# A first stage in another order: the third attention unit ahead of the second up step, and weight conversion further ahead

## The chip, the cores and the metric

The kernel runs on one core of one Trainium2 chip. The metric is the device time of one execution in microseconds (us). The engines are TensorE (PE in the profile, PEld for its weight loads), VectorE (DVE), ScalarE (ACT), GpSimd (POOL) and SyncE (SP, which issues most transfers). Each has a program of its own.

## The reference

A retention block without softmax feeds a multiplicative feed-forward network:

```python
scores = scale * np.matmul(q, k.transpose(0, 1, 3, 2))
ret = scores * Dmat[None, :, :, :]            # decay gamma ** (i - j) below the diagonal, 0 above
x = np.matmul(ret, v)                         # (8, 8, 576, 64), turned to (4608, 512)
a = x @ w1; b = x @ w2
out = ((a * b) @ w3) @ w_out                  # w1, w2: 512 x 1024; w3: 1024 x 1024; w_out: 1024 x 512
```

The weights come as float64: the kernel reads them as pairs of 32-bit integers and makes float32 of them itself.

## The kernel before

The sequence is cut into units of up to 128 positions (five to a pair of batches). A unit is loaded, its q and v are scaled on GpSimd (`scale`), q and k are transposed on TensorE and copied out by ScalarE (`front`), a running state is updated (`state`), scores are made on TensorE and masked on VectorE (`score`), and `pv` multiplies with v. The up step `up(pair, token block, weight part)` is a Strassen product: seven products on TensorE, adds on VectorE. It needs sums S1 to S4 of converted weight blocks; a weight part has four blocks. It also needs sums of x, the token sums, which `strassen_tokens` makes for each token block.

A block is converted in five steps, which a generator hands out wherever the kernel calls `convert(n)`:

```python
def begin_block():                             # three steps
    vec.tensor_scalar(out=e, in0=hi, ...)      # exponent field
    yield
    vec.tensor_scalar(out=m, in0=hi, ...)      # mantissa, high part
    yield
    vec.scalar_tensor_tensor(m, in0=lo, ..., in1=m)
    nc.scalar.activation(e, e, relu, ...)      # two activations on ScalarE
    nc.scalar.activation(e, e, relu, ...)
    yield

def end_block():                               # two steps; after the fourth block of a part, the sums too
    vec.scalar_tensor_tensor(e, in0=hi, ..., in1=e)
    yield
    vec.scalar_tensor_tensor(out, in0=m, ..., in1=e)
    ...                                        # next load; strassen_weights
    yield

def conversion():
    yield from begin_block()
    while converted[0] < len(blocks):
        if begun[0] < len(blocks):
            yield from begin_block()
        yield from end_block()
```

`conv=2` in an up step hands out two conversion steps after each of its adds and at its end. The adds go through one tile `c` with a single buffer: ScalarE copies the first product into it, VectorE adds the others, multiplies (`ab`), and only then can the next up step use it.

Of the kernel before, what the change touches and what calls it, by code (L numbers as in the profile page):

```python
# [32 lines left out]
def kernel(  # L33
# [124 lines left out]
    def scale(g, nm):  # L158
        c = g % NC
        sz = sizes[c]  # L160
        t, gam = live[nm, g], {"q": gq, "v": gk}[nm]
        t = t[:sz].rearrange("p (b h) d -> p b h d", b=2)
        nc.gpsimd.tensor_tensor(  # L163
            out=t, in0=t, in1=gam[:sz, c].unsqueeze(1).unsqueeze(3).to_broadcast([sz, 2, H, D]), op=ALU.mult)

    def front(g):
        c = g % NC
        sz = sizes[c]
        kn, qn = live["k", g], live["q", g]
        kT = pools["fr"].tile([P, 2, NP, P], F32, tag="kT", name="kT", bufs=1)  # L170
        qT = pools["fr"].tile([P, 2, NP, P], F32, tag="qT", name="qT")
        for src, dst in ((kn, kT), (qn, qT)):
            for b in range(2):
                tp = acc.tile([P, NP, P], F32, tag="acc", name="tp")
                for p in range(NP):
                    h = b * H + 2 * p
                    nc.tensor.transpose(tp[:, p, :sz],  # L177
                                        src[:sz, h:h + 2, :].rearrange("p a d -> p (a d)"),
                                        ident[:sz, :sz])
                nc.scalar.copy(dst[:, b, :, :sz], tp[:, :, :sz])  # L180
        live["kT", g], live["qT", g] = kT, qT
# [17 lines left out]
    def state(g):  # L199
        c = g % NC  # L200
        sz = sizes[c]
        if c == NC - 1:
            return
        kn, vs = live["k", g], live["v", g]
        if c == 0:
            live["st"] = st_ps.tile([P, 2, NP, D], F32, tag="st", name="st")
        st = live["st"]

        for b in range(2):
            for p in range(NP):  # L210
                for j, hs in enumerate(heads):
                    h = b * H + 2 * p + j
                    nc.tensor.matmul(st[hs, b, p, :], kn[:sz, h, :], vs[:sz, h, :],  # L213
                                     start=(c == 0 and b == 0 and p == 0), stop=(c == NC - 2),
                                     skip_group_check=True)
        sb = pools["fr"].tile([P, 2, NP, D], F32, tag="sb", name="sb")
        nc.scalar.copy(sb, st)
        live["sb", g + 1] = sb
# [32 lines left out]
    blocks = []  # L251
# [7 lines left out]
    loaded, begun, converted, turned = [0], [0], [0], [0]  # L259
# [23 lines left out]
    def converted_to(n):  # L283
        key, _ = blocks[n]
        if key[0] == "w12":
            _, fp, j, r = key
            return wA[fp // 2][:, j, 2 * r:2 * r + 2, fp % 2 * QC:fp % 2 * QC + QC]
        if key[0] == "wo":
            return live["wo"][:, key[1], :]
        _, ft, g0 = key  # L290
        if ("w3", ft) not in live:
            live["w3", ft] = pools["wst"].tile([P, DF], F32, tag="w3", name="w3")
        return live["w3", ft][:, g0:g0 + CV]

    def begin_block():
        n = begun[0]
        t = live["raw", n]
        lo, hi = t[:, :, 0], t[:, :, 1]
        e = raw.tile([P, CV], I32, tag="exp", name="e")
        m = raw.tile([P, CV], I32, tag="man", name="m")  # L300
        vec = nc.vector


        vec.tensor_scalar(out=e, in0=hi, scalar1=1, scalar2=21,  # L304
                          op0=ALU.logical_shift_left, op1=ALU.logical_shift_right)
        yield

        vec.tensor_scalar(out=m, in0=hi, scalar1=0x000FFFFF, scalar2=0x00100000,
                          op0=ALU.bitwise_and, op1=ALU.bitwise_or)
        yield  # L310
        vec.scalar_tensor_tensor(m.bitcast(F32), in0=lo.bitcast(U32), scalar=2.0 ** -32, in1=m,  # L311
                                 op0=ALU.mult, op1=ALU.add)
        relu = mybir.ActivationFunctionType.Relu
        nc.scalar.activation(e, e, relu, bias=lim[:, 0:1], scale=-1.0)  # L314
        nc.scalar.activation(e, e, relu, bias=lim[:, 1:2], scale=-2.0 ** 23)
        live["em", n] = e, m
        begun[0] += 1
        yield

    def end_block():  # L320
        n = converted[0]
        hi = live["raw", n][:, :, 1]
        e, m = live["em", n]
        vec = nc.vector
        vec.scalar_tensor_tensor(e, in0=hi, scalar=-(1 << 31), in1=e,  # L325
                                 op0=ALU.bitwise_and, op1=ALU.bitwise_or)
        yield
        key = blocks[n][0]
        while not (key[0] == "w12" or "wo" in live and (key[0] == "wo" or key[1] < turned[0] + 2)):
            yield "wait"  # L330
        out, m, e = converted_to(n), m.bitcast(F32), e.bitcast(F32)
        if key[0] == "w12":
            m, e = (x.rearrange("p (c n) -> p c n", c=2) for x in (m, e))
        vec.scalar_tensor_tensor(out, in0=m, scalar=2.0 ** -20, in1=e, op0=ALU.mult, op1=ALU.mult)  # L334
        converted[0] += 1

        if n > 0:
            load_block()
        if key[0] == "w12" and key[1] > 0 and key[2:] == (1, 1):
            yield from strassen_weights(key[1])  # L340
        yield

    def conversion():

        yield from begin_block()
        while converted[0] < len(blocks):
            if begun[0] < len(blocks):
                yield from begin_block()
            yield from end_block()

    converting = [conversion()]

    def go_on():
        while converting:
            r = next(converting[-1], "end")
            if r != "end":
                return r
            converting.pop()
        return "end"

    def convert(n):

        for _ in range(n):
            if go_on() is not None:
                return
# [28 lines left out]
    def has_x(i, n):  # L394
        return any(starts[c] + sizes[c] >= (n + 1) * TB and ("x", i * NC + c) in live for c in range(NC))
# [17 lines left out]
    def up(i, n, fp, conv=0):  # L413
        m = every.index((i, n))
        while ("S", fp) not in live:
            assert go_on() is None
        if ("B", i, n) not in live:
            strassen_tokens(i, n)
        if fp == 0:
            live["ab", i, n] = (pools["ab3"] if m == 2 else ffn).tile([P, 2 * KF, TB], F32, tag="ab", name="ab")  # L420
        ab = live["ab", i, n]

        def product(ps, a, b):
            a, b = A(fp, a), live["B", i, n][b]
            new = ps is None
            if new:
                ps = acc.tile([P, 2, TB], F32, tag="acc", name="up")
            for w in range(2):
                for r in range(2):
                    nc.tensor.matmul(ps[:, w, :], a[:, w, r, :], b[:, r, :], start=(new and w == r == 0),  # L430
                                     stop=(w == r == 1), skip_group_check=True)
            return ps

        def plus(ps, to, sb):
            nc.vector.tensor_add(c[:, to], ps, c[:, sb])  # L435
            convert(conv)


        c = ffn.tile([P, 4, 2, TB], F32, tag="c", name="c", bufs=1)
        p1 = product(None, "A11", "B11")  # L440
        nc.scalar.copy(c[:, 0], p1)  # L441
        plus(product(None, "S2", "T2"), 1, 0)
        plus(product(None, "S3", "T3"), 2, 1)
        p5 = product(None, "S1", "T1")
        plus(p5, 3, 2)
        plus(product(None, "A22", "-T4"), 2, 2)
        product(p1, "A12", "B21")
        nc.scalar.copy(c[:, 0], p1)  # L448
        product(p5, "S4", "B22")
        plus(p5, 1, 1)  # L450

        if fp == NQ - 1 and m + 1 < len(every) and has_x(*every[m + 1]) and ("B", *every[m + 1]) not in live:
            strassen_tokens(*every[m + 1])
        nc.vector.tensor_mul(ab[:, 4 * fp:4 * fp + 4, :], c[:, :, 0, :], c[:, :, 1, :])  # L454
        convert(conv)
# [43 lines left out]
    scale(1, "q")  # L499
    front(1)  # L500
    scale(1, "v")
    state(1)
    score(1)
    convert(2)
    pv(1)
    strassen_tokens(0, 0, nc.vector)
    load(3, "kqv")
    up(0, 0, 0, conv=2)
    scale(2, "q")
    scale(2, "v")  # L510
    up(0, 0, 1, conv=2)
    front(2)
    state(2)
    score(2)
    load(4, "k")
    scale(3, "q")
    front(3)
    scale(3, "v")
    load(4, "q")
    state(3)  # L520
    score(3)
# [1 line left out]
    load(4, "v")  # L523
    pv(3)
    strassen_tokens(0, 1, nc.vector)
    convert(2)
    up(0, 1, 0, conv=2)
    scale(4, "q")
    scale(4, "v")
# [136 lines left out]
```

## Time and profile before

| | |
|---|---|
| time, median of 6 runs | 938.4 us (937.4 to 939.0) |
| span of the profiled run | 935.2 us |
| TensorE busy | 899.6 us (96%) |
| TensorE idle from 0 to 30 us, where DMA is full | 15.9 us |
| TensorE idle from 40 to 60 us, where VectorE is full | 10.7 us |

The last two rows are the lengths of the windows less TensorE's busy time in them; the prediction shows the windows. Besides these large gaps TensorE has small ones later; three of them are of one kind. This is its order in time (start us, duration us, engine, line, operation, matrices, count; in brackets the idle time ahead of the group and who ended it):

```profile
108.31 1.57 PE L430 MATMUL up<-xT,wS 128*128 128x192 f32 x8 [0.78 <-DVE c L435]
...
120.43 1.57 PE L430 MATMUL up<-xT,wS 128*128 128x192 f32 x8 [0.57 <-DVE c L435]
...
143.07 1.57 PE L430 MATMUL up<-xT,wS 128*128 128x192 f32 x8 [1.05 <-DVE c L435]
```

Each is the last product of an up step. It accumulates onto a bank of PSUM, the memory that TensorE writes its products to, and VectorE must first have read that bank in an earlier add. Together they are 0.78 + 0.57 + 1.05 = 2.4 us.

### The profile page before, as it was taken

What the parts mean: (1) busy time and instruction counts of PE and PEld (TensorE: products, weight loads), DVE (VectorE), ACT (ScalarE), POOL (GpSimd) and SP (SyncE); (2) the same over time, 40 slices, a digit from 0 to 9 for tenths busy, and PEclk for the clock granted to TensorE, in tenths of its full rate; (3) what the DMA queues carried; (4) which work ended last, traced back from release to release, by engine and by line L of the source; (5) the groups of instructions that cost most, each with busy time, mean ns of one, the idle gap of its engine ahead of it and who ended that gap; (6) DMA issues with size and microseconds to landing.
All of it is one profiled execution on the core that took longest, in us unless ns stands there. A gap on an engine that the chain in (4) does not pass through costs nothing.

```text
span 935.2 us, 14109 instructions
## 1 busy us (share of the span) xinstructions
PE 899.6 (96%) x6085; PEld 712.6 (76%) x6085; DVE 351.9 (38%) x597; ACT 202.5 (22%) x373; POOL 118.4 (13%) x87
## 2 busy tenths in 40 slices
PE   4859999999999999999999999999999999999998
PEld 3758999955446769968968968959958959789593
DVE  4786989877001213412312312403313404224030
ACT  4324433445113322111111111111121110011010
POOL 2311001000301333103002120003020101000000
PEclk9979999999999999999999999999999999999999
DMA  9944323232616653304013213134010000000101
GB/s 197 221 122 105 113 69 112 92 113 68 101 34 136 126 90 69 69 12 91 1 35 66 38 35 68 23 68 80 1 46 13 1 28 7 12 23 1 34 1 34
DMA packets 125550, 59.67 MB, mean 64 GB/s; under 512 B 113704, under 2 KB 113704, under 8 KB 125488
## 3 DMA queue, kind: packets, MB, share of 16 engines
q1 hardware_dynamic: 123824, 58.47, 27.8%
q8 instruction: 48, 0.79, 0.4%
q10 hardware_dynamic: 1664, 0.30, 0.2%
q14 instruction: 14, 0.11, 0.0%
HBM read 49.32 MB, written 9.44 MB: 63 GB/s over the span
## 4 chain that ended last, share of the span: by engine, by line
PE 90%; DVE 5%; DMA 2%; issue 1%; ACT 1%; SPq 1%; DVEq 0%
PE up L430 43%; PE po L461 27%; PE ps L387 6%; PE sc L192 4%; PE xps L241 4%; PE tp L177 3%; PE xps L234 2%; PE st L213 2%; SPq L101 1%; DVE c L435 1%; DVE e L325 1%; DMA ld_v<-in_v_dram 1%; DMA raw<-in_moe_w_dram 1%; PE tp L377 1%; DVE m L311 0%
## 5 line engine op out<-in xcount | busy, mean ns | idle before, releaser
L435 DVE TENSOR_TENSOR c<-up,c 128x384 f32<-128x384 f32 x240 | 133.5, 556 | 338.7 <-PE up L430 334.6
L461 PE MATMUL po<-w3o,ab 128*128 128x512 f32 x576 | 251.0, 593 | 0.0
L430 PE MATMUL up<-xT,wA 128*128 128x192 f32 x1152 | 213.4, 328 | 9.0 <-DVE wA L334 7.4
L461 PEld LDWEIGHTS po<-w3o,ab 128*128 128x128 f32 x576 | 108.2, 190 | 129.2 <-issue 128.4
L430 PEld LDWEIGHTS up<-xT,wA 128*128 128x128 f32 x1152 | 191.4, 191 | 13.5 <-DVE wA L334 7.7
L430 PE MATMUL up<-T,wS 128*128 128x192 f32 x768 | 142.0, 328 | 4.1 <-DVE wS L148 2.7
L430 PEld LDWEIGHTS up<-T,wS 128*128 128x128 f32 x768 | 128.4, 191 | 4.9 <-issue 4.8
L195 DVE TENSOR_TENSOR pm<-sc,mask 128x512 f32<-128x512 f32 (+1 forms) x80 | 45.5, 629 | 187.6 <-PE sc L192 181.1
L430 PE MATMUL up<-xT,wS 128*128 128x192 f32 x384 | 70.8, 327 | 2.8 <-DVE c L435 2.7
L163 POOL TENSOR_TENSOR ld_q<-ld_q,gq 128x1024 f32<-128x1024 f32 (+1 forms) x20 | 38.2, 1912 | 272.8 <-DMA ld_q<-in_q_dram 267.4
L464 ACT COPY ot<-po 128x512 f32<-128x512 f32 x36 | 21.1, 586 | 238.6 <-PE po L461 238.6
L448 ACT COPY c<-up 128x384 f32<-128x384 f32 x48 | 22.9, 478 | 225.7 <-PE up L430 222.9
L163 POOL TENSOR_TENSOR ld_v<-ld_v,gk 128x1024 f32<-128x1024 f32 (+1 forms) x20 | 38.6, 1931 | 253.3 <-DMA ld_v<-in_v_dram 245.6
L430 PE MATMUL up<-T,wA 128*128 128x192 f32 x384 | 70.2, 326 | 0.0
L430 PEld LDWEIGHTS up<-xT,wS 128*128 128x128 f32 x384 | 63.4, 190 | 4.3 <-DVE c L435 4.3
L430 PEld LDWEIGHTS up<-T,wA 128*128 128x128 f32 x384 | 63.7, 190 | 0.0
L387 PE MATMUL ps<-wo,w3T 128*128 128x512 f32 x128 | 56.3, 592 | 0.0
L454 DVE TENSOR_TENSOR ab<-c 128x768 f32<-128x768 f32 x48 | 46.3, 965 | 3.8
L314 ACT ACTIVATE e<-e,lim 128x512 int32<-128x512 int32 x40 | 28.8, 721 | 72.8 <-DVE e L304 72.8
L387 PEld LDWEIGHTS ps<-wo,w3T 128*128 128x128 f32 x128 | 23.7, 190 | 26.8 <-issue 26.8
L192 PE MATMUL sc<-qT,kT 64*128 64x128 f32 (+1 forms) x640 | 39.9, 278 | 1.8 <-ACT qT L180 1.8
L441 ACT COPY c<-up 128x384 f32<-128x384 f32 x48 | 22.9, 477 | 79.6 <-DVE ab L454 54.9
(51 smaller groups left out, 568.6 us busy)
## 6 DMA issues: line engine op xcount, KB each, us to landing
raw<-in_moe_w_dram SPq DMA_DIRECT2D x24, 512.0 KB, 3.7
ld_k<-in_k_dram SPq DMA_DIRECT2D x16, 512.0 KB, 6.4
ld_q<-in_q_dram SPq DMA_DIRECT2D x16, 512.0 KB, 7.3
ld_v<-in_v_dram SPq DMA_DIRECT2D x16, 512.0 KB, 4.6
out_dram<-ot SPq DMA_DIRECT2D x24, 256.0 KB, 2.0
raw<-in_moe_w_dram SPq DMA_DIRECT2D x16, 256.0 KB, 6.3
raw<-in_moe_w_out_dram SPq DMA_DIRECT2D x8, 512.0 KB, 3.6
out_dram<-ot SPq DMA_DIRECT2D x24, 128.0 KB, 2.4
```

Source lines behind the costliest of these rows:

```text
L163: nc.gpsimd.tensor_tensor(out=t, in0=t, in1=gam[:sz, c].unsqueeze(1).unsqueeze(3).to_broadcast([sz, 2, H, D]), op=ALU.mult)
L177: nc.tensor.transpose(tp[:, p, :sz], src[:sz, h:h + 2, :].rearrange("p a d -> p (a d)"), ident[:sz, :sz])
L192: nc.tensor.matmul(sc[j][:sz, p, :sz], kT[hs, b, p, :sz], qT[hs, b, p, :sz], start=True, stop=True)
L195: nc.vector.tensor_mul(pm[:sz, b, j, :, :sz], sc[j][:sz, :, :sz], mask[:sz, :sz].unsqueeze(1).to_broadcast([sz, NP, sz]))
L241: nc.tensor.matmul(banks[r][heads[half], b, n, :sz], vs[:sz, b * H + 2 * p + j, :], pm[:sz, b, j, p, :sz], start=(c == 0 and m == 0), stop ...
L314: nc.scalar.activation(e, e, relu, bias=lim[:, 0:1], scale=-1.0)
L387: nc.tensor.matmul(ps, live["w3T", ft][:, g, :], live["wo"][:, g, :], start=(g == 0), stop=(g == KF - 1))
L430: nc.tensor.matmul(ps[:, w, :], a[:, w, r, :], b[:, r, :], start=(new and w == r == 0), stop=(w == r == 1), skip_group_check=True)
L435: nc.vector.tensor_add(c[:, to], ps, c[:, sb])
L441: nc.scalar.copy(c[:, 0], p1)
L454: nc.vector.tensor_mul(ab[:, 4 * fp:4 * fp + 4, :], c[:, :, 0, :], c[:, :, 1, :])
L461: nc.tensor.matmul(po, ab[:, f, t * P:(t + 1) * P], live["w3o"][:, f, :], start=(f == 0), stop=(f == KF - 1))
```

## The change

It wants TensorE's work of unit 2 to lie in the time in which the second up step waits for its weights, and VectorE to use its own wait for block 4.

```diff
     def conversion():
         yield from begin_block()
         while converted[0] < len(blocks):
-            if begun[0] < len(blocks):
+            if begun[0] < len(blocks) and converted[0] != 3:
                 yield from begin_block()
             yield from end_block()
+            if begun[0] == converted[0] < len(blocks):
+                yield from begin_block()
...
     scale(1, "v")
+    convert(8)
     state(1)
     score(1)
-    convert(2)
     pv(1)
     strassen_tokens(0, 0, nc.vector)
     load(3, "kqv")
     up(0, 0, 0, conv=2)
     scale(2, "q")
     scale(2, "v")
-    up(0, 0, 1, conv=2)
     front(2)
     state(2)
     score(2)
     load(4, "k")
     scale(3, "q")
+    scale(3, "v")
+    up(0, 0, 1, conv=2)
     front(3)
-    scale(3, "v")
     load(4, "q")
...
     pv(3)
     strassen_tokens(0, 1, nc.vector)
-    convert(2)
     up(0, 1, 0, conv=2)
```

## The prediction

> **What bounds the kernel now.** I read the page's busy shares and slices first, then the windows of 10 us, then the orders in time of TensorE, VectorE and GpSimd up to 220 us.
>
> ```profile
> PE 899.6 (96%) x6085; PEld 712.6 (76%) x6085; DVE 351.9 (38%) x597; ACT 202.5 (22%) x373; POOL 118.4 (13%) x87
> ...
> PE   4859999999999999999999999999999999999998
> ...
> PEclk9979999999999999999999999999999999999999
> ```
>
> TensorE is busy for 899.6 of 935.2 us; only 35.6 us are open. The windows say where they lie. Columns: stretch, its length, then busy us of PE, PEld, DVE, ACT, POOL, granted clock, DMA share, GB/s.
>
> ```profile
> 0.00:10.00 10.00, 2.71 (x21) 2.40 (x21) 0.44 (x5) 2.29 (x4) 3.73 (x9) 1.00 0.90 156
> 10.00:20.00 10.00, 5.90 (x100) 5.61 (x99) 9.01 (x19) 6.09 (x12) 1.00 (x1) 1.00 1.11 237
> 20.00:30.00 10.00, 5.49 (x48) 4.50 (x46) 5.15 (x10) 3.92 (x7) 3.80 (x2) 1.00 1.01 231
> 30.00:40.00 10.00, 9.30 (x112) 8.42 (x112) 8.29 (x13) 3.48 (x8) 1.84 (x1) 1.00 1.19 201
> 40.00:50.00 10.00, 7.66 (x44) 7.09 (x44) 9.93 (x13) 2.35 (x4) 5.90 (x4) 1.00 1.09 226
> 50.00:60.00 10.00, 1.65 (x4) 1.14 (x4) 9.76 (x16) 3.25 (x5) 0.72 (x1) 0.69 0.58 151
> ```
>
> Ten less the PE column gives 15.9 us idle in 0:30, 0.7 in 30:40, 2.3 in 40:50 and 8.35 in 50:60. The first 30 us are a DMA stretch (share about 1), which the change does not touch. In 40:60 the DMA is no longer the limit; VectorE is (9.93 and 9.76 of 10). TensorE's order in time shows for what it waits:
>
> ```profile
> 47.77 0.81 PE L430 MATMUL up<-xT,wA 128*128 128x192 f32 x4
> 55.98 1.65 PE L430 MATMUL up<-xT,wA 128*128 128x192 f32 x4 [7.39 <-DVE wA L334]
> 60.38 2.90 PE L430 MATMUL up<-T,wS 128*128 128x192 f32 x8 [2.75 <-DVE wS L148]
> 63.07 1.90 PE L430 MATMUL up<-xT,wA 128*128 128x192 f32 x8
> 64.81 1.46 PE L430 MATMUL up<-T,wS 128*128 128x192 f32 x8
> ```
>
> The second up step needs weight blocks 4 to 7 converted and their sums (S1 to S4) made on VectorE: 7.39 + 2.75 = 10.1 us of wait. Independent work (the front of unit 2, its state and scores) stands behind that step in TensorE's program. Earlier, VectorE itself waits:
>
> ```profile
> 21.40 0.69 DVE L334 SCALAR_TENSOR_TENSOR wA<-m,e 128x512 f32<-128x512 f32 x1
> ...
> 22.43 1.90 POOL L163 TENSOR_TENSOR ld_q<-ld_q,gq 128x1024 f32<-128x1024 f32 x1 [11.43 <-DMA ld_q<-in_q_dram]
> ...
> 26.77 0.43 DVE L304 TENSOR_SCALAR e<-raw 128x512 int32<-128x512 int32 x1 [4.68 <-DMA raw<-in_moe_w_dram]
> ```
>
> After block 2 it begins block 4, whose load lands at 26.7 us, although block 3 could have been finished at 22.1.
>
> **What the Trainium skill says.** "TensorE: Matmul & The Clock Gate", section "What's actually happening": after an idle window of about 3.4 us the array clock is halved, and comes back after about as long a busy one. The trace agrees: after the 10 us gap two groups of 8 took 2.90 and 1.90 us against 1.46, with a granted clock of 0.69 in 50:60. Starts put this at 64.81 - 60.38 = 4.43 us for two groups that elsewhere start 1.30 apart, so 1.8 us lost. "SBUF — State Buffer", section "SBUF: two separate sides": VectorE with two SBUF inputs and GpSimd exclude each other for a whole instruction. The trace agrees:
>
> ```profile
> 37.73 0.56 DVE L404 TENSOR_TENSOR T<-xT,T 128x384 f32<-128x384 f32 x1
> 38.16 1.90 POOL L163 TENSOR_TENSOR ld_q<-ld_q,gq 128x1024 f32<-128x1024 f32 x1 [11.76 <-DMA ld_q<-in_q_dram]
> 38.21 2.27 DVE L404 TENSOR_TENSOR xT<-xT 128x384 f32<-128x384 f32 x1
> ```
>
> The same shape took 2.27 beside GpSimd and 0.56 alone. Four such meetings between 37 and 52 us (2.27 for 0.56, 2.38, 2.27 and 1.92 for 0.69) cost 6.2 us together, 1.55 each. The first-named page, section "Architectural detail", calls VectorE and ScalarE strict FIFO, so what counts is program order on each, which I followed through the generator by hand.
>
> **The change part by part.** Steps of VectorE from its order in time, start to start: beginning a block 1.41 us (26.77 to 28.18), ending it 1.44 (28.18 to 29.62), four sums 2.7, four masks 2.5, an add 0.47, the product ab 0.87.
>
> (a) *Block 3 no longer waits for block 4.* VectorE goes on at 22.1 instead of 26.77: up to 4.7 us. But there the two scalings of unit 1 on GpSimd run (22.43 and 24.50, 1.90 each), which hit an idle VectorE before and now meet the end of block 3 and S1. Two meetings at 1.55 are 3.1 us. Block 3 and sums: 22.1 + 1.44 + 2.7 + 3.1 = 29.3, against 32.3 before.
>
> (b) *Eight steps ahead of the masks of unit 1*: begin 4, begin 5, end 4 are 4.26 us, so the masks run from 33.6 to 36.1, against 32.3 to 35.0. Loads: block 4 landed at 26.7; block 5, next in the queue at some 2.3 us for 512 KB, about 29.0 (estimate from 512 KB at 231 GB/s). They are wanted at 29.3 and 30.7, so neither load holds VectorE up. The scores are ready sooner, as ScalarE copies the transposes without first doing block 4's exponents (it did those at 27.23, the copies at 28.61). But pv of unit 1 ends on the last masks: half of its 1.9 us after 36.1, then the 0.6 us copy: tokens start at 37.65, against 37.07. So this early part gives nothing and costs 0.6 us; what it buys is work done ahead: one end, and one third step, of a block less to do later.
>
> (c) *Third unit before the second step.* From the tokens to S2 of the second step VectorE was without a gap, 37.07 to 60.2 = 23.1 us. Now it has end 4 (1.44) and the last part of begin 5 (0.61) less, and the four masks of unit 2 (2.5) more: 23.1 + 0.45 = 23.6. The meetings with GpSimd stay four. S2 is done at 37.65 + 23.6 = 61.2, so the second step's second product starts at 61.3, against 60.38: 0.9 us later. But front, state and scores of unit 2 are then behind TensorE. They took 70.01 to 74.91 = 4.9 us before, and they now lie in the gap. Left of the gap: the first step ends at about 48.2, unit 2 runs to about 53.7 (behind the copies of ScalarE), A11 to 55.6, then 5.7 us idle. That is still over an idle window, so I leave the 1.8 us of half clock in.
>
> (d) *Load order.* Block 8 now stands ahead of unit 3's loads and holds them 2.3 us; unit 3's tiles are wanted only after the second step. Unit 4's q arrives sooner, and its scaling meets VectorE at about 70 us, which has slack there (6.3 us idle before the masks of unit 3, from 76.6).
>
> (e) *Later.* The order from up(0,1,0) on is the same with the conversion two steps (1.1 us) behind, as one convert(2) is gone. TensorE's waits there are small: 0.78 at 108.31, 0.57 at 120.43, 1.05 at 143.07. The sums now fall behind the last add rather than ahead of it, and I expect some 0.5 us of these waits to go.
>
> Sum: 4.9 - 0.9 + 0.5 = 4.5 us. Everything after is a full TensorE, so it reaches the end whole: 937.7 - 4.5 = 933.2.
>
> **Rivals.** *The gap closes altogether.* If (a) meets no lock (masks done at 34.4, tokens at 35.9), S2 comes at 59.5 and the gain is 6.2; if in addition the clock stays up, 8.0: 929.7. For it: GpSimd's spans are rough, and masks and adds from PSUM are not slowed by it (an add at 48.88 took 0.54 beside a scaling). Against it: all four meetings of two-SBUF-input operations in this stretch show the delay. *VectorE is the bound and takes all back.* The masks of unit 2 lie in its full stretch; if two more meetings fall there (3.1 us), S2 comes at 64.4 and the gain is 1.4: 936.3. For it: 9.9 of 10 busy. Against it: the number of scalings in the stretch is the same. *The last wait is a transfer.* Blocks 5 to 7 or unit 3 land late and hold conversion or scaling. For it: DMA share about 1 to 50 us. Against it: after 26.77 no conversion of the kernel before waited long for a load. It would cost about one load, 2.3 us: 935.5. *Later conversions miss their step*: two steps behind, against S(3) finished 20 us before its step at about 144 us. It would cost under 1 us.
>
> **Range and chances.** The rivals span 929.7 to 936.3, and repeat runs 937.37 to 938.84; I take 929.5 to 936.3. Two per cent are 18.8 us, nearly all that TensorE's idle time from 40 us on and the clock loss hold (2.3 + 8.35 + 0.4 + 1.9 + 2.4 up to 150 us, 3.6 after, 1.8 clock = 20.8), so faster by that much is all but excluded; slower by as much would need a new stall that nothing here shows.
>
> **What would show it.** In the trace after: VectorE's end of block 3 at 22.1 and stretched operations beside the scalings at 22 to 27; the masks of unit 1 at about 33.6; tokens near 37.7; unit 2's transposes at about 48; the second step's S2 product near 61.3 at half clock; and everything from up(0,1,0)'s second product (89.94 before) about 4 us earlier. I am wrong if tokens start before 36 or after 39, if that product is not 2 to 7 us earlier, or if TensorE waits anew after 90 us.

## The result

The changed kernel took 929.8 us (929.3 to 931.3, 6 runs), against 938.4: 8.6 us less. Ratios here are the mean time of one kernel's fast runs over that of the other's of the same rounds, so not quite the ratio of the medians; this one is 0.9913, with a 95% interval of 0.9900 to 0.9925. By the 2% rule the two are the same; the difference is clear of noise all the same. The spans of the profiled runs differ by 935.2 - 927.6 = 7.6 us.

The page's lines on TensorE, after:

```profile
PE 897.5 (97%) x6085; PEld 711.2 (77%) x6085; DVE 352.8 (38%) x597; ACT 202.6 (22%) x373; POOL 118.8 (13%) x87
...
PE   4869999999999999999999999999999999999998
...
PEclk9989999999999999999999999999999999999999
```

The same 6085 matmuls lie in a span 7.6 us shorter. The third slice of 23 us is no longer at 5 but at 6, and its clock at 8 instead of 7. TensorE's order in time there:

```profile
45.48 1.57 PE L433 MATMUL up<-xT,wS 128*128 128x192 f32 x8 [0.15 <-DVE c L438]
46.88 1.04 PE L177 MATMUL tp<-ident,ld_k 128*128 128x128 f32 x8
47.76 1.04 PE L177 MATMUL tp<-ident,ld_q 128*128 128x128 f32 x8
48.72 1.15 PE L213 MATMUL st<-ld_v,ld_k 128*64 128x64 f32 x32
49.87 2.06 PE L192 MATMUL sc<-qT,kT 64*128 64x128 f32 x32
51.86 1.57 PE L433 MATMUL up<-xT,wA 128*128 128x192 f32 x8
60.56 2.90 PE L433 MATMUL up<-T,wS 128*128 128x192 f32 x8 [7.13 <-DVE wS L148]
```

Unit 2's transposes, state and scores run right behind the first up step without a wait. Then one wait of 7.13 us is left in place of two of 7.39 and 2.75. The product that ends it starts at 60.56, against 60.38 before, and runs at half clock as before.

VectorE ends block 3 without waiting for block 4, and meets GpSimd's scalings instead. All engines in order of time, the changed kernel:

```profile
21.89 0.68 DVE L325 SCALAR_TENSOR_TENSOR e<-raw,e 128x512 int32<-128x512 int32 x1
...
22.61 0.69 DVE L334 SCALAR_TENSOR_TENSOR wA<-m,e 128x512 f32<-128x512 f32 x1
...
23.11 1.95 POOL L163 TENSOR_TENSOR ld_q<-ld_q,gq 128x1024 f32<-128x1024 f32 x1 [12.24 <-DMA ld_q<-in_q_dram]
23.34 2.27 DVE L148 TENSOR_TENSOR wS<-wA 128x512 f32<-128x512 f32 x1
...
25.21 2.15 POOL L163 TENSOR_TENSOR ld_v<-ld_v,gk 128x1024 f32<-128x1024 f32 x1 [0.16 <-DMA ld_v<-in_v_dram]
...
25.64 2.27 DVE L148 TENSOR_TENSOR wS<-wS,wA 128x512 f32<-128x512 f32 x1
```

The sums S1 and S2 took 2.27 us each beside a scaling; S3 and S4, with none beside them, took 0.68.

Where the gain arises is seen from the same events in both traces:

| event, us from the start of the span | before | after | difference |
|---|---|---|---|
| token sums of block 0 start on VectorE | 37.07 | 37.22 | +0.15 |
| second product of the second up step | 60.38 | 60.56 | +0.18 |
| token sums of block 1 start | 86.99 | 82.10 | -4.89 |
| second product of the step after it | 89.94 | 84.98 | -4.96 |
| first product with w3 (`ps`) | 191.20 | 183.54 | -7.66 |
| end | 935.2 | 927.6 | -7.6 |

Five microseconds are gained ahead of 90 us, where the unit was moved; the experiments below show that it takes the early part of the change too. The other 2.7 come after 90 us, where the order of TensorE's work was not changed. The page's groups of instructions (busy us, mean ns, then TensorE's idle time ahead of the group and what ended most of it) have this line before:

```profile
L430 PE MATMUL up<-xT,wS 128*128 128x192 f32 x384 | 70.8, 327 | 2.8 <-DVE c L435 2.7
```

and this after:

```profile
L433 PE MATMUL up<-xT,wS 128*128 128x192 f32 x384 | 70.7, 328 | 0.2 <-DVE c L438 0.2
```

The three small waits on VectorE's add are gone.

### The profile page after: what moved, and what is told of

It is laid out like the page before. It is cut to its first block, busy times and chain, and to the rows that moved or that the text cites. A ratio compares the mean times of both kernels' runs of the same rounds, so it can differ in the third digit from the quotient of the medians.

```text
span 927.6 us, 14109 instructions
## 1 busy us (share of the span) xinstructions
PE 897.5 (97%) x6085; PEld 711.2 (77%) x6085; DVE 352.8 (38%) x597; ACT 202.6 (22%) x373; POOL 118.8 (13%) x87
## 4 chain that ended last, share of the span: by engine, by line
PE 92%; DVE 5%; issue 1%; DMA 1%; ACT 0%; SPq 0%; DVEq 0%
PE up L433 46%; PE po L464 27%; PE ps L390 6%; PE xps L241 3%; PE sc L192 3%; PE tp L177 3%; PE xps L234 2%; PE st L213 1%; DMA raw<-in_moe_w_dram 1%; DVE e L325 1%; PE tp L380 1%; DVE wS L148 1%; DVE pm L195 1%; DVE wA L334 1%; DVE m L311 0%
## 5 line engine op out<-in xcount | busy, mean ns | idle before, releaser
L241 PE MATMUL xps<-pm,ld_v 128*64 128x128 f32 (+1 forms) x640 | 37.9, 270 | 1.5 <-DVE pm L195 1.4
```

What stands on the lines that cost most here:

```text
L241: nc.tensor.matmul(banks[r][heads[half], b, n, :sz], vs[:sz, b * H + 2 * p + j, :], pm[:sz, b, j, p, :sz], start=(c == 0 and m == 0), stop ...
```

## The experiments

The ratios are against the kernel before on the same chip, five rounds each. "Three groups" is the time from the start of the second step's second product to that of the fifth, three groups of products later, which at full clock is 3 x 1.30 = 3.9 us.

| run | median us | ratio, 95% interval | second product starts | three groups |
|---|---|---|---|---|
| before | 938.4 | 1 | 60.38 | 5.73 |
| changed kernel | 929.8 | 0.9913, 0.9900 to 0.9925 | 60.56 | 5.62 |
| changed kernel, again | 929.9 | 0.9913, 0.9901 to 0.9926 | 61.22 | 5.47 |
| two steps put back | 933.2 | 0.9948, 0.9933 to 0.9963 | 60.63 | 6.12 |
| only the two steps out | 934.6 | 0.9966, 0.9952 to 0.9981 | 61.00 | 5.68 |
| only unit 2 moved | 937.4 | 0.9995, 0.9980 to 1.0010 | 64.29 | 6.21 |
| only the early part | 935.4 | 0.9969, 0.9953 to 0.9985 | 58.15 | 6.98 |
| block 4 first | 931.5 | 0.9926, 0.9914 to 0.9938 | 63.05 | 5.38 |
| masks first | 931.3 | 0.9927, 0.9915 to 0.9939 | 60.45 | 6.82 |
| scalings of unit 1 on VectorE | 929.9 | 0.9918, 0.9904 to 0.9931 | 60.97 | 5.37 |
| more in the gap | 925.8 | 0.9868, 0.9855 to 0.9881 | 64.24 | 3.9 |
| masks first and more in the gap | 926.2 | 0.9879, 0.9865 to 0.9893 | 62.33 | 3.9 |

**The control.** The changed kernel once more, beside three other runs.

> The changed kernel unaltered, once more, so that the three runs beside it are compared with it on the same chip. Expected: about 8.6 us faster than before (ratio 0.991), and TensorE's second product of the second step at 60.5 us.

929.9 us and 0.9913 again; the second product came at 61.22, 0.7 later than in the other trace. That much lies between two profiles of one kernel.

**The two steps put back.** Into the changed kernel:

```diff
     strassen_tokens(0, 1, nc.vector)
+    convert(2)
     up(0, 1, 0, conv=2)
```

> The changed kernel with the two conversion steps put back ahead of the first up step of the second token block, so that from there on every engine has the order of the kernel before. Theory: 5.0 us of the gain of 7.6 us (profiled spans) come from the unit moved into the gap, and the other 2.6 us from TensorE's waits at 108, 120 and 143 us in the kernel before (0.78, 0.57, 1.05 us, on VectorE's add), which the two-step shift of the conversion against ScalarE's copies takes away. Then this run must have those three waits back and be 2.0 to 2.8 us slower than the changed kernel: span about 930.0, time about 932.2. Rival: the waits went because VectorE had done more by then (the masks of unit 2 earlier); then they stay away, and the run is within 0.7 us of the changed kernel, about 929.8.

It took 933.2 us. TensorE's order in time has the three waits again, to within 0.02 us:

```profile
103.93 1.57 PE L433 MATMUL up<-xT,wS 128*128 128x192 f32 x8 [0.79 <-DVE c L438]
116.05 1.57 PE L433 MATMUL up<-xT,wS 128*128 128x192 f32 x8 [0.56 <-DVE c L438]
138.69 1.57 PE L433 MATMUL up<-xT,wS 128*128 128x192 f32 x8 [1.05 <-DVE c L438]
```

The loss of 3.3 us (929.9 to 933.2, two sessions) is more than their 2.4, and more than the 2.0 to 2.8 expected; in this trace the half clock also took 0.5 us more (6.12 for 5.62). The theory stands as to the two steps, and the rival falls: two steps of conversion, 1.1 us of VectorE's work, decide on these waits.

How they do is seen, for the first wait, on ScalarE. In the kernel before:

```profile
100.95 0.72 ACT L314 ACTIVATE e<-e,lim 128x512 int32<-128x512 int32 x1 [3.76 <-DVE e L304]
101.70 0.72 ACT L315 ACTIVATE e<-e,lim 128x512 int32<-128x512 int32 x1
102.33 1.05 ACT L180 COPY kT<-tp 128x512 f32<-128x512 f32 x2
103.27 1.08 ACT L180 COPY qT<-tp 128x512 f32<-128x512 f32 x2
104.22 0.51 ACT L441 COPY c<-up 128x384 f32<-128x384 f32 x1
```

and in the changed kernel:

```profile
93.49 1.07 ACT L180 COPY kT<-tp 128x512 f32<-128x512 f32 x2 [0.78 <-PE tp L177]
94.45 1.10 ACT L180 COPY qT<-tp 128x512 f32<-128x512 f32 x2
97.83 0.48 ACT L444 COPY c<-up 128x384 f32<-128x384 f32 x1 [2.28 <-DVE ab L457]
98.20 0.72 ACT L314 ACTIVATE e<-e,lim 128x512 int32<-128x512 int32 x1
```

Before, ScalarE first waited 3.76 us for VectorE to begin a block, did its two activations, then the four copies of unit 4's transposes, and only then the first copy into `c`, for which VectorE's adds of that step waited. After, the activations stand behind that copy, and the copies of the transposes start as soon as TensorE has made them. VectorE's first add of the step, before and after:

```profile
104.77 0.56 DVE L435 TENSOR_TENSOR c<-up,c 128x384 f32<-128x384 f32 x1 [1.92 <-ACT c L441]
```

```profile
98.34 0.56 DVE L438 TENSOR_TENSOR c<-up,c 128x384 f32<-128x384 f32 x1 [0.26 <-ACT c L444]
```

The change took no work away; it took a wait out of ScalarE's order.

The other two waits have no such line. Ahead of the second, at 120.43, VectorE worked without a gap from 104.77 on, so it may still have been late from the first; that is argued. Ahead of the third, at 143.07, conversion ran beside GpSimd's token sums (before, then after):

```profile
139.60 1.00 POOL L404 TENSOR_TENSOR T<-xT,T 128x384 f32<-128x384 f32 x1 [1.39 <-PE up L430]
139.74 1.41 DVE L325 SCALAR_TENSOR_TENSOR e<-raw,e 128x512 int32<-128x512 int32 x1
```

```profile
132.91 0.67 DVE L311 SCALAR_TENSOR_TENSOR m<-raw,m 128x512 f32<-128x512 uint32 x1
133.03 1.41 POOL L407 TENSOR_TENSOR T<-xT,T 128x384 f32<-128x384 f32 x1 [1.13 <-ACT e L314]
```

Before, the step between the first two adds began after GpSimd's sum and took 1.41 us; after, another step stood there, began first and took 0.67. The third add came 3.21 us after the first before (139.26 to 142.47) and 2.48 after (132.44 to 134.92), which is 0.73 of the 1.05 us. The run with the two steps put back has the 1.41 again, and the next run, with them out, 0.68. So two steps in another place changed what VectorE met, besides what ScalarE did first.

**Only the two steps out** of the kernel before:

```diff
     strassen_tokens(0, 1, nc.vector)
-    convert(2)
     up(0, 1, 0, conv=2)
```

> The kernel before with nothing changed but those two conversion steps taken out. Theory (order of conversion against ScalarE alone): the three waits go here as well, 2.0 to 2.8 us faster than before, about 935.9. Rival (VectorE's earlier lead is needed too): less than 0.7 us, about 938. Second rival: two steps fewer leave later sums late for their step, and a new wait on VectorE's sums appears at 100 to 150 us: slower than before.

934.6 us, ratio 0.9966: about 3.2 us, a little more than the 2.0 to 2.8 expected, which its interval (1.8 to 4.5 us) takes in. The trace has none of the three waits; counted from the token sums of block 0, the first product with w3 comes 2.65 us earlier (189.01 - 37.53 against 191.20 - 37.07). No late sums appear. So this one deleted line is worth more than a third of the whole gain, by itself.

**Only unit 2 moved** in the kernel before:

```diff
-    up(0, 0, 1, conv=2)
     front(2)
     state(2)
     score(2)
     load(4, "k")
     scale(3, "q")
+    scale(3, "v")
+    up(0, 0, 1, conv=2)
     front(3)
-    scale(3, "v")
```

> The kernel before with unit 2's front, state and scores ahead of the second up step, and nothing else: conversion as before. Theory: the 4.9 us of TensorE's work go into the gap, and the four masks (2.4 us) on VectorE put the second step's sums off by as much: its second product starts at about 62.8 (60.4 before), net gain 2.5 us, time about 935.9. Rival: the masks are hidden, or meet no full VectorE, and the whole 4.9 us are gained (933.5).

937.4 us, ratio 0.9995: nothing clear of noise, where 2.5 us were expected, and neither theory nor rival had this. TensorE's order in time, then ScalarE's:

```profile
54.14 3.78 PE L192 MATMUL sc<-qT,kT 64*128 64x128 f32 x32 [5.04 <-ACT qT L180]
```

```profile
45.59 0.46 ACT L448 COPY c<-up 128x384 f32<-128x384 f32 x1
51.16 0.72 ACT L314 ACTIVATE e<-e,lim 128x512 int32<-128x512 int32 x1 [5.11 <-DVE e L304]
51.91 0.72 ACT L315 ACTIVATE e<-e,lim 128x512 int32<-128x512 int32 x1
52.54 1.05 ACT L180 COPY kT<-tp 128x512 f32<-128x512 f32 x2
```

Unit 2's transposes were done by 48 us, but their copies stood behind the activations of block 7, and ScalarE idled 5.11 us until VectorE had begun that block. So the scores waited 5.04 us, and VectorE, whose next work was their masks, stood idle too:

```profile
56.24 1.29 DVE L195 TENSOR_TENSOR pm<-sc,mask 128x512 f32<-128x512 f32 x2 [2.71 <-PE sc L192]
```

The second step's sums were late, its second product at 64.29 rather than the expected 62.8, and of the 4.9 us only 0.6 were left (the token sums of block 1 start at 86.43, for 86.99 before).

**Masks first.** The unit moved as above, with the two later steps out, and in the early stage only this:

```diff
     score(1)
-    convert(2)
+    convert(5)
     pv(1)
```

> The kernel before with unit 2 moved, three conversion steps more AFTER the masks of unit 1 (five for two), the two later steps out; block 4 still begun ahead of the end of block 3. It tells why moving unit 2 alone gained nothing. Theory: there ScalarE's copies of unit 2's transposes stood behind the exponents of block 7, which VectorE had not begun (a wait of 5.0 us for the scores); the three steps bring block 7 forward, the wait goes, and the run is 6 to 8 us faster than before, 930.5 to 932.5, without the early part of the change. Rival: the wait came from VectorE's total work; then the three steps more ahead of the tokens only delay them (tokens at 37.7), and the scores of unit 2 wait over 3 us again: over 934.

931.3 us, ratio 0.9927, inside the expectation. The scores no longer wait, and the second product starts at 60.45. TensorE's order in time:

```profile
48.75 1.15 PE L213 MATMUL st<-ld_v,ld_k 128*64 128x64 f32 x32
49.90 2.06 PE L192 MATMUL sc<-qT,kT 64*128 64x128 f32 x32
```

Three steps of conversion more ahead of the first up step bring block 7 forward enough for ScalarE; neither the new rule in the generator nor the place ahead of the masks is needed for that. Of the 1.4 us to the control's median the two traces show 0.6 (spans of 928.7 and 928.1 us): the half clock took 1.35 us more here (6.82 for 5.47), and the second product came 0.77 earlier. The rest stays open, and the intervals overlap.

**Only the early part**, that is the generator's new rule and the eight steps ahead of the masks of unit 1 in place of the two behind them, in the kernel before.

```diff
+            if begun[0] < len(blocks) and converted[0] != 3:
...
+    convert(8)
     state(1)
     score(1)
-    convert(2)
```

> The kernel before with the early part alone: block 3 finished without waiting for block 4, and eight conversion steps ahead of the masks of unit 1; no unit moved, the two later steps kept. Theory: tokens start where they did (37.1 to 37.3), but VectorE has about 2.1 us less to do in the stretch after, so the second step's second product starts at about 57.9 (60.4 before) and the gain is 2.4 us, about 936.0. Rival: the stretch from 37 us is bound by the landing of loads or by the meetings with GpSimd, and the work done ahead buys nothing: within 0.7 us of before.

935.4 us, ratio 0.9969, near the expectation. The second product starts at 58.15, 2.2 us earlier; 1.25 of these were lost again in the profiled run to the half clock (6.98 for 5.73). With the other runs this divides the five microseconds ahead of 90 us. By the ratios the early part alone is worth 2.9 us, the unit alone 0.5, and both together, which is the run with the two steps put back (0.9948), 4.9. So the unit adds about 2.0 us to the early part; the early part adds 4.4 to the unit.

**Block 4 first.** The changed kernel with the old generator and five steps in place of eight, so that only the order of block 4's beginning and block 3's end is undone.

```diff
-            if begun[0] < len(blocks) and converted[0] != 3:
+            if begun[0] < len(blocks):
...
-    convert(8)
+    convert(5)
```

> The changed kernel with block 4 begun ahead of the end of block 3 again (as before), five steps in place of eight at the place ahead of the masks of unit 1, so that after it the order is that of the changed kernel. Theory: VectorE idles from about 22 to 26.7 us for the load of block 4 and then has the same work; masks of unit 1 about 2 us later (35.2 for 33.2), and as nothing after has slack until the second step, everything is about 2 us later: about 931.9. Rival: the meetings with GpSimd that the new order runs into (4.54 us for two sums of 0.69) eat what the wait cost, and the run is within 0.7 us of the changed kernel.

931.5 us against 929.9 beside it. The masks of unit 1 start at 35.60, the second product at 63.05, 1.8 us later. The intervals of the two ratios overlap (0.9914 to 0.9938 and 0.9901 to 0.9926), so the time alone doesn't settle it; the shift in the trace is as the theory has it. Once the steps stand ahead of the masks, the generator's rule is worth 1.6 us by the medians and 1.8 by the traces, one of each.

**Scalings of unit 1 on VectorE**, to see whether the long sums are the meeting with GpSimd:

```diff
-    scale(1, "q")
+    scale(1, "q", nc.vector)
     front(1)
-    scale(1, "v")
+    scale(1, "v", nc.vector)
```

> The changed kernel with the two scalings of unit 1 on VectorE instead of GpSimd, so that nothing meets the sums of the first step. Theory (meetings with GpSimd delay VectorE): the two sums that took 2.27 us each take 0.69, VectorE pays about 2.3 us for the scalings itself, and its masks of unit 1 begin 0.5 to 1.2 us earlier than 33.2 to 33.3; time 0.3 to 1 us below the changed kernel, within its noise (about 929.3). Rival (the 2.27 us are something else, as the queue's order or the load): the sums stay long, VectorE is 2.3 us later, and so is the end (932).

VectorE's order in time:

```profile
23.21 0.69 DVE L148 TENSOR_TENSOR wS<-wA 128x512 f32<-128x512 f32 x1
23.94 0.69 DVE L148 TENSOR_TENSOR wS<-wS,wA 128x512 f32<-128x512 f32 x1
...
25.75 1.22 DVE L163 TENSOR_TENSOR ld_q<-ld_q,gq 128x1024 f32<-128x1024 f32 x1
```

The sums are short, so the rival falls: each meeting had cost 1.58 us. A scaling on VectorE costs 1.14 from start to start, little less, and q is ready later; the masks (32.95) waited 0.49 us for the scores, the token sums started at 37.33, and the time is that of the changed kernel (929.9). So the masks began only 0.2 us earlier than in the changed kernel, where 0.5 to 1.2 were expected, and the 0.3 to 1 us of time did not come.

**More in the gap.** The changed kernel, with front and state of unit 3 and `pv` of unit 2 ahead of the second up step as well:

```diff
+    front(3)
+    state(3)
+    pv(2)
     up(0, 0, 1, conv=2)
-    front(3)
     load(4, "q")
-    state(3)
     score(3)
-    pv(2)
     load(4, "v")
```

> The changed kernel with more work in the remaining gap: front and state of unit 3 and pv of unit 2 (1.75 + 1.08 + 2.9 us) ahead of the second up step too. VectorE's order is unchanged. Theory: TensorE had 7.1 us of idle time there and loses 1.7 us to the half clock after it; the second product still starts at 60.5, at full clock, and the gain is 5.7 to 7.4 us over the changed kernel: 922.4 to 924.1. Rival: ScalarE's order turns against it (the copies of pv of unit 2 now stand ahead of the exponents of block 8 and of the first copy of the second step), the first add waits, and half of it or more is lost: over 926.

925.8 us, ratio 0.9868: it beats both kernels, by 4.1 us the changed one. That is less than the expected 5.7 to 7.4; the time lies between the theory's 922.4 to 924.1 and the rival's over 926. TensorE's order in time:

```profile
56.67 0.65 PE L177 MATMUL tp<-ident,ld_q 128*128 128x128 f32 x4 [1.89 <-DVE pm L195]
...
58.43 1.99 PE L234 MATMUL xps<-qT,sb 64*64 64x128 f32 x32
...
64.24 1.46 PE L433 MATMUL up<-T,wS 128*128 128x192 f32 x8
```

The gap is full and the second product runs at full clock. But it starts at 64.24, not 60.5: unit 2 began 1.4 us later than in the changed kernel's trace (48.27 for 46.88), the last transposes of unit 3 waited 1.89 us for a PSUM bank that the scores of unit 2 held until VectorE had masked them, and `pv` then ran at half clock (1.99 us for 32 matmuls that take 1.10 elsewhere). The named rival, ScalarE's order, was not what cost it in this trace. The profiled execution was the slowest of the four, though: 927.5 us, with a mean granted clock of 0.989, against 925.4 to 925.9 and 0.994 to 0.998. Its span is only 1.8 us below that of the changed kernel, so what the half clock cost in the other three is not shown.

**Masks first and more in the gap.** On top of "masks first", with the old generator:

```diff
+    front(3)
+    state(3)
+    pv(2)
     up(0, 0, 1, conv=2)
-    front(3)
     load(4, "q")
-    state(3)
     score(3)
-    pv(2)
```

> The run with the masks of unit 1 ahead of the three conversion steps, with the order of the run with more work in the gap: the generator of conversion stays as in the kernel before. Theory: the early part of the change is not needed, so this is as fast as the run with more in the gap (925.8) within 1 us, perhaps 0.5 to 1 us faster as VectorE had its sums for the second step 0.8 us earlier. Rival: the early part carries something that only shows once the gap is filled; over 927.5.

926.2 us, ratio 0.9879, within 1 us of 925.8 as the theory has it: the changed generator is not needed here either. In this trace `pv` kept the full clock (1.10 us) after a wait of 0.86 us in the place of 1.89, and the second product came at 62.33; it too is of the slowest of four executions (927.6 us). The 0.5 to 1 us more that the theory thought possible did not come.

## Why the prediction was right, and where it was not

The time, 929.8, lies in the range, near its lower end; the gain was 8.6 us where 4.5 were predicted. That it is nearly the first rival's 929.7 is chance: the gap did not close, and the gain came from elsewhere. By the prediction's parts:

- **The bound, right.** The TensorE gap from 48 to 60 us was the place, VectorE's conversion the cause, and the early DMA stretch did not move.
- **(a) and (b), right in mechanism.** Block 3 ended at once, two operations met the scalings (S1 and S2, not the end of block 3 and S1), at 1.58 us each where 1.55 was reckoned. The Trainium skill's page "SBUF — State Buffer", section "SBUF: two separate sides", says so of operations with two SBUF inputs, and the run with the scalings moved shows it. Masks came at 33.2 (33.6 predicted), tokens at 37.22 (37.65).
- **(c), right in the sum, mis-sized by 0.7 us, and incomplete.** The second product was 0.18 us late, where 0.9 was predicted, and the whole 4.9 us of TensorE's work were hidden. Of the 0.7, 0.4 are (b)'s earlier tokens; for the rest, the four meetings cost 5.1 us (1.00 for 0.43, 1.92 and 2.26 for 0.69, 2.67 for 0.95), not 6.2, while VectorE waited 0.85 for TensorE. The prediction took from (b) two conversion steps less for VectorE. What it did not see is how much this step depends on (b): alone, moving unit 2 gained nothing clear of noise, as ScalarE's copies stood behind activations of a block not begun. The prediction quoted strict FIFO from the Trainium skill's page "TensorE: Matmul & The Clock Gate", section "Architectural detail", and followed ScalarE's order for unit 1, but for unit 2 it only noted that it runs behind ScalarE's copies and did not ask what these stand behind. The second rival ("VectorE takes all back") is near to what happened in that run, by another way.
- **(d), right on the loads, wrong on the meeting.** Unit 3's tiles were scaled 1.9 and 2.8 us later (48.20 and 51.25, for 46.28 and 48.48), where 2.3 was predicted. Unit 4's q was scaled at 76.56, not at about 70, and delayed nothing there.
- **(e), the step that failed in size.** "I expect some 0.5 us of these waits to go": all of 2.4 went, and the trace gained 2.7 us there. The single-line run gives it without the rest of the change. The prediction read the waits as VectorE being late, by sums ahead of an add. The first wait came through ScalarE, whose copy into `c` stood behind activations and transposes (VectorE waited 1.92 us for it, then 0.26); at the third, GpSimd's token sums drew out a conversion step (1.41 us for 0.69); the second was not settled.
- **The clock, right.** The gap left was 7.13 us, where 5.7 was predicted, still over an idle window, and the second product ran at half speed; the first rival's closed gap did not come. It came in "more in the gap", with a loss elsewhere.

Sum of what was measured: 4.9 - 0.2 + 0.2 + 2.7 = 7.6 us in the profiled runs, the second 0.2 being the stretch between the second product and the next tokens. The medians differ by 1.0 us more than the spans; the spread of single runs, 1.6 to 2.0 us in each kernel, covers that, and no experiment divides it.

What stays open is how much the half clock differs from run to run in the executions that were not profiled.

## What to carry to other kernels

When engines work in order, moving one engine's work moves the place of the work that it hands to the others: follow each engine's own queue past the move, ScalarE's copies as well as the busy engine. A copy that frees or feeds something should not stand behind an activation whose input another engine has yet to make; two small conversion steps in another place were worth 3 us here, in part by this. And parts of a change need not add up: unit 2's move was worth nothing clear of noise without three steps of conversion ahead of it.

## What the Trainium skill lacked or had wrong

- "TensorE: Matmul & The Clock Gate", section "What's actually happening", gives about 3.4 us idle as what halves the clock. That agreed with the 7 us gap. But in "more in the gap" `pv` ran at half speed (1.99 us for 1.10, granted clock 0.50 from 59 to 61 us) after a wait of only 1.89 us, and the clock fell to 0.50 again from 80 to 82 us after waits of 1.36 and 0.17 us; in "masks first and more in the gap" waits of 1.36 and 0.16 us in the same place did not bring it down. Which activity the gate had counted there, no run shows.
- The same section says that the return to full clock takes about 3.4 us of work and varies with the window's phase. Here, after 6.5 to 7.2 us of waiting, three groups took 5.37 to 6.82 us, against 3.9 at full clock: 1.5 to 2.9 us were lost, which at half speed is 2.9 to 5.8 us of work (an estimate: twice the loss). The longest is well above the page's figure; in "masks first" the granted clock was 0.50 from 61 to 66 us.
- "SBUF — State Buffer", section "SBUF: two separate sides", was right that two-input operations are held up. For VectorE's side of such a meeting it has one figure, 6.8 times slower, without a shape; here a sum of 0.69 us took 2.27, 3.3 times as long, beside a scaling of 1.95 us. A conversion step with one input, `e<-raw`, was drawn out as well: 1.00 us for 0.43 at 40.71 us in the changed kernel, 2.12 at 53.56 us in "more in the gap".
- "TensorE: Matmul & The Clock Gate", section "Architectural detail", states ScalarE's FIFO order in one line and not what it can cost. Here it was 5.04 us for one unit's scores, which waited for copies whose inputs were ready.
